# Seven block products instead of eight in two layers of an attention and expert kernel, second and third pass

## The chip, the core and the metric

One core of a Trainium2 chip runs the whole program. The metric is the device time of one execution in microseconds (us). The engines are TensorE (PE, with PEld for its weight loads), VectorE (DVE), ScalarE (ACT), GpSimd (POOL), and SyncE (SP), which issues the DMA transfers.

## What is computed

Attention over 2 x 8 heads of 768 rows of 64, masked to pairs with the same hash of six signs; its output, 1536 rows of 512, goes through two dense layers:

```python
x = attn_out.transpose(0, 2, 1, 3).reshape(1536, 512)
x = ((x @ w_a) * (x @ w_b)) @ w_out        # 512 -> 1536 -> 512, "expert layers", "expert output"
h = x @ w_in                               # 512 -> 2048, "hidden layer"
out = np.maximum(0.01 * h, h) @ w_out2     # 2048 -> 512, "last layer"
```

## The kernel before

The rows after attention are worked on in three passes of 512. The first runs between the attention tiles; the second and third come after it, with PE alone on the dense layers. Every product is made in three matmuls: each operand is split into a rounded part (fp32r, names ending in h) and the rest (names ending in l), and h·h, l·h and h·l are accumulated (`three`, L710, and `out_products`, L797). A weight unit is 128 x 512 numbers; `weights` (L361) loads it from a copy in DRAM (`kept`), rounds it on ACT or DVE (`wh`), and subtracts on DVE or POOL (`wl`).

`moe` (L735) computes, per pass, 12 pairs of blocks of the expert layers (24 x 12 matmuls), gates and splits them (`gh`, `gl`), and then the expert output, 4 blocks of 36 matmuls; `moe2` (L783) the hidden layer, 16 blocks of 12 with a leaky relu, split into `hh` and `hl`, and the last layer, 16 chunks of 12. All these matmuls stream 512 columns. Results stand in six PSUM banks (`psM`, `psN`) used in turn.

Nothing is issued by hand: `Plan` (L41) collects operations with engine, estimated length and due time, and `issue` (L103) orders them once, at build time; rings (`RINGS`) limit how many buffers of a name are alive. Each engine then runs its own list in that order and waits on semaphores.

Of the kernel before, what the change touches and what calls it, by code (L numbers as in the profile page):

```python
# [19 lines left out]
UT = 256  # L20
# [7 lines left out]
}  # L28


# [6 lines left out]
    "LATE": 10, "STIR": 24, "by": {"act": -610.0, "dve": 16.0, "pool": -157.0},  # L37
}


# [156 lines left out]
def lsh_attention_moe_kernel(  # L197
# [34 lines left out]
    wp = ctx.enter_context(tc.tile_pool(name="wp", bufs=1))  # L232

    NA = 2 * NB
    eye = const.tile([128, 128], F32, name="eye")
# [91 lines left out]

    first = list(w_units())
    NU = len(first)
    kept = [dram.tile([128, 512], F32, name="kept%d" % i) for i in range(NU)] if wide else None  # L330

    plan = Plan()
    op = plan.op
    T, P = {}, {"wp": wp}
    SP, PE, ACT, DVE, POOL = "sp", "pe", "act", "dve", "pool"
    eng = {DVE: dve, POOL: pool}

# [23 lines left out]
    def alloc(*news):  # L361
        return [n for n, _ in news], lambda f: (lambda *e: ([m() for _, m in news], f(*e)))

    def weights(i, b, at):
# [3 lines left out]
        if wide and b == 0:  # L368
# [30 lines left out]
            def f_add():  # L399
# [19 lines left out]
            op(SP, 360, lambda: sp.dma_start(out=kept[i], in_=T["w32", k]), at - 8500, "keep",  # L419
               reads=[("w32", k)], writes=[("kept", i)], uses=[("w32", k)], lag=3500)  # L420
        else:
            n, f = alloc(w32)
# [283 lines left out]
    def tick(ns):  # L706
        clock["at"] += ns * clock["pace"]
        return clock["at"]

    def three(ps, w, x, reads, uses, first, last, new_ps):  # L710

        for kt in range(4):
            def emit(kt=kt):
                hi, lo = (T[k].rearrange("p (c f) -> p c f", c=4)[:, kt] for k in w)
                mh, ml = x(kt)
                o = T[ps]
                pe.matmul(o, hi, mh, start=first and kt == 0, stop=False)  # L717
                pe.matmul(o, hi, ml, start=False, stop=False)  # L718
                pe.matmul(o, lo, mh, start=False, stop=last and kt == 3)  # L719

            nn, f = alloc(*(new_ps if kt == 0 else []))
            op(PE, 3 * MM, f(emit), tick(3 * MM), "m" if kt == 0 else None,
               reads=list(w) + reads(kt), writes=[ps], new=nn,
               uses=list(w) + uses + ([] if nn else [ps]))

    def two(names, p, pool, n, ring=None):

# [2 lines left out]

    def bank_m(ring, key):
        r = next(ring)
        return [new(r, [128, 512], F32, key, "m", r)]

    def moe(p, ring, x_reads):  # L735
        unit = iter(range(NU))
# [46 lines left out]
    def moe2(p, ring):  # L783
        unit = iter(range(NU - 2 * KH, NU))
        yh, yl, hh, hl = ((x, p) for x in ("yh", "yl", "hh", "hl"))
        for f in range(KH):
            w = weights(next(unit), p, clock["at"])
            ps, tk = ("ph", p, f), ("h32", p, f)
            three(ps, w, lambda kt: (T[yh][:, kt], T[yl][:, kt]),
                  lambda kt: [yh + (kt,), yl + (kt,)], [yh, yl], True, True,  # L790
                  bank_m(ring, ps))
            op(ACT, 600, lambda ps=ps: act.activation(T[ps], T[ps], AF.Lrelu, alpha=0.01),
               clock["at"], reads=[ps], writes=[tk], uses=[ps])
            split(ps, tk, hh, hl, f, two(("hh", "hl"), p, "h", KH) if f == 0 else [], True)
        NT = PT // 128

        def out_products(f, i, w):  # L797
            ps, ts = ("po", p, i), slice(i * 128, (i + 1) * 128)

            def emit():  # L800
                wh, wl = T[w[0]], T[w[1]]
                pe.matmul(T[ps], T[hh][:, f, ts], wh, start=f == 0, stop=False)  # L802
                pe.matmul(T[ps], T[hh][:, f, ts], wl, start=False, stop=False)  # L803
                pe.matmul(T[ps], T[hl][:, f, ts], wh, start=False, stop=f == KH - 1)  # L804

            nn, al = alloc(*(bank_m(ring, ps) if f == 0 else []))
            op(PE, 3 * MM, al(emit), tick(3 * MM), "m", reads=list(w) + [hh + (f,), hl + (f,)],
               writes=[ps], new=nn, uses=list(w) + [hh, hl] + ([] if nn else [ps]))

        LAST = KH - 2  # L810
        for f in range(LAST):
            w = weights(next(unit), p, clock["at"])
            for i in range(NT):
                out_products(f, i, w)
        ws = {f: weights(next(unit), p, clock["at"] + (f - LAST) * 3 * MM)
              for f in range(LAST, KH)}
        for i in range(NT):
            for f in range(LAST, KH):
                out_products(f, i, ws[f])
            g, c = divmod(p * PT // 128 + i, KT)  # L820
            dst = out[g * S:(g + 1) * S, :].rearrange("(p c) e -> p c e", p=128)[:, c, :]
            ps, ot = ("po", p, i), ("ot", p, i)
            nn, al = alloc(new("o", [128, 512], F32, ot, "o"))
            op({ACT: 600, DVE: 690}, 0, al(lambda e, ps=ps, ot=ot: rounded(e, T[ot], T[ps])),
               clock["at"], reads=[ps], writes=[ot], new=nn, uses=[ps])
            op(SP, 600, lambda dst=dst, ot=ot: sp.dma_start(out=dst, in_=T[ot]),
               clock["at"], reads=[ot], uses=[ot], lag=2000)

    def reload(p, at):

        full, xh, xl = ("x32f", p), ("xh", p), ("xl", p)
        n, f = alloc(new("xx", [128, KX, PT], F32, full, "x32f"))
        op(SP, 600, f(lambda: sp.dma_start(out=T[full], in_=xd[p])), at, "xl",
           reads=[("xd", p, c, o) for c in range(KX) for o in range(0, PT, UT)], writes=[full],
           new=n, lag=5000)
        for c in range(KX):
            n, f = alloc(*([new("xx", [128, KX, PT], F32R, key, nm, ring=nm)
                            for key, nm in ((xh, "xh1"), (xl, "xl1"))] if c == 0 else []))
            us = [full] if n else [full, xh, xl]
            op(ACT, 630, f(lambda c=c: act.activation(T[xh][:, c], T[full][:, c], AF.Copy)),  # L840
               at + 9000, "xs", reads=[full], writes=[xh + (c,)], new=n, uses=us)
            op({POOL: 1300, DVE: 692}, 0, lambda e, c=c: eng[e].tensor_tensor(
                out=T[xl][:, c], in0=T[full][:, c], in1=T[xh][:, c].bitcast(F32),
                op=ALU.subtract), at + 10000, "xd", reads=[full, xh + (c,)], writes=[xl + (c,)],
               uses=[full, xh, xl], lock=True)


    def pools(stack, space, **bufs):
        for n, b in bufs.items():
            P[n] = stack.enter_context(tc.tile_pool(name=n, bufs=b, **space))  # L850

    with tc.manual_schedule():
        outer, right, left, psum, psb = (ExitStack() for _ in range(5))
        in_psum = {"space": PSUM}
        on_right = {"side": "right"}
        pools(outer, on_right, edge=1)
        P["edge"].tile([128, 248], F32, name="edge")
        pools(right, on_right, pw=1, raw=1, km=1, qs=1, e=1, pt=1, st=1)
        pools(left, {}, x=1, t=1, g=1)
# [42 lines left out]
        clock["at"], clock["pace"] = start2 + PAR["START"], PAR["PACE"]  # L902
        moe(0, cycle(["psM"]), xs0)

        def free_banks():
            psb.close()
            pools(psb, {**in_psum, **on_right}, psN=1, psP=1)

        def free_right():
            right.close()  # L910
            pools(right, on_right, o=1, xx=1, h=1)

        sw3 = op("host", 0, free_banks, 0, after=plan.ring_users("B") + plan.ring_users("Sa"))
        sw2 = op("host", 0, free_right, 0, after=list(range(n_att)))
        plan.ring("psN", 4, sw3)
        plan.ring("mp", 2, sw3)
        for r in ("x32f", "xh1", "xl1", "hh", "hl"):
            plan.ring(r, 1, sw2)
# [12 lines left out]
        right.close()  # L931
# [33 lines left out]
```

## Time and profile before

| | us |
|---|---|
| median of 3 runs | 815.25 (815.14 to 815.39) |
| the profiled execution | 815.48 |
| its span, first to last instruction | 813.8 |
| PE / DVE / ACT / POOL busy | 802.5 / 462.5 / 510.8 / 194.5 |
| second and third pass on PE | 440.1 to 810.1 |

A page has the engines' busy times, the span in 40 slices, DMA queues, the chain that ended last, and groups of instructions by line. An engine's busy share is an average over the span, so it is read by stretches. Matmuls are pipelined: the recorded length of one (0.39 us) is longer than the distance to the next.

### The profile page before, as it was taken

What the parts mean: (1) busy time and instruction counts of PE and PEld (TensorE: products, weight loads), DVE (VectorE), ACT (ScalarE), POOL (GpSimd) and SP (SyncE); (2) the same over time, 40 slices, a digit from 0 to 9 for tenths busy, and PEclk for the clock granted to TensorE, in tenths of its full rate; (3) what the DMA queues carried; (4) which work ended last, traced back from release to release, by engine and by line L of the source; (5) the groups of instructions that cost most, each with busy time, mean ns of one, the idle gap of its engine ahead of it and who ended that gap; (6) DMA issues with size and microseconds to landing.
All of it is one profiled execution on the core that took longest, in us unless ns stands there. A gap on an engine that the chain in (4) does not pass through costs nothing.

```text
span 813.8 us, 12310 instructions
## 1 busy us (share of the span) xinstructions
PE 802.5 (99%) x4248; PEld 657.0 (81%) x4248; DVE 462.5 (57%) x757; ACT 510.8 (63%) x969; POOL 194.5 (24%) x295
## 2 busy tenths in 40 slices
PE   7999999999999999999999999999999999999998
PEld 6787887878878778778888888888888888888886
DVE  6665776767858766568984454355422544335421
ACT  7887898888878777879864444256423444246522
POOL 3222344443544343438861000000000000000000
PEclk9999999999999999999999999999999999999999
DMA  4354664676766554578785333432334323333332
GB/s 107 91 123 125 166 182 121 180 226 212 196 179 199 166 160 155 164 237 288 258 289 181 104 91 99 148 100 95 97 98 145 101 95 100 96 99 94 100 91 77
DMA packets 96926, 118.76 MB, mean 146 GB/s; under 512 B 31936, under 2 KB 63328, under 8 KB 96608
## 3 DMA queue, kind: packets, MB, share of 16 engines
q1 hardware_dynamic: 96064, 117.78, 48.1%
q8 instruction: 33, 0.54, 0.3%
q10 hardware_dynamic: 800, 0.20, 0.1%
q14 instruction: 29, 0.24, 0.1%
HBM read 82.84 MB, written 23.07 MB: 130 GB/s over the span
## 4 chain that ended last, share of the span: by engine, by line
PE 93%; ACT 2%; DVE 2%; POOL 1%; issue 1%; DMA 0%; POOLq 0%; ACTq 0%; DVEq 0%
PE m L717 17%; PE m L718 17%; PE m L719 17%; PE S L583 8%; PE B L663 8%; PE B L621 7%; PE m L804 5%; PE m L802 5%; PE m L803 5%; PE B L520 2%; ACT e L599 1%; PE B L674 1%; DVE st L587 1%; PE B L488 1%; DMA kept<-w 0%
## 5 line engine op out<-in xcount | busy, mean ns | idle before, releaser
L341 ACT ACTIVATE wh<-w 128x512 fp32r<-128x512 f32 x188 | 118.6, 631 | 209.8 <-PE m L718 112.7
L438 DVE TENSOR_TENSOR wl<-w,wh 128x512 fp32r<-128x512 f32 x172 | 122.8, 714 | 173.6 <-ACT wh L341 173.3
L717 PE MATMUL m<-xh,wh 128*128 128x512 f32 x480 | 190.0, 396 | 1.0 <-DVE hl L778 1.0
L718 PE MATMUL m<-xl,wh 128*128 128x512 f32 x480 | 187.1, 390 | 0.0
L719 PE MATMUL m<-xh,wl 128*128 128x512 f32 x480 | 187.0, 390 | 0.0
L587 DVE TENSOR_REDUCE st<-S 128x1 f32<-128x768 f32 x96 | 91.8, 957 | 44.0 <-PE S L583 42.0
L599 ACT ACTIVATE e<-S,st 128x768 f32<-128x768 f32 x96 | 95.3, 992 | 19.9 <-POOL st L594 15.7
L400 POOL TENSOR_TENSOR w<-m,r 128x512 uint32<-128x512 uint32 x68 | 90.7, 1335 | 65.4 <-ACT r L390 22.1
L719 PEld LDWEIGHTS m<-xh,wl 128*128 128x128 f32 x480 | 90.2, 188 | 19.2
L717 PEld LDWEIGHTS m<-xh,wh 128*128 128x128 f32 x480 | 90.2, 188 | 19.0 <-DVE hl L778 1.4
L718 PEld LDWEIGHTS m<-xl,wh 128*128 128x128 f32 x480 | 90.3, 188 | 17.5
L341 ACT ACTIVATE P<-B 128x384 f32<-128x384 f32 x187 | 82.2, 489 | 16.9 <-PE B L621 16.2
L621 PE MATMUL B<-eye,e 128*128 128x128 f32 x576 | 79.3, 274 | 0.0
L802 PE MATMUL m<-wh,hh 128*128 128x512 f32 x192 | 74.7, 389 | 0.0
L803 PE MATMUL m<-wl,hh 128*128 128x512 f32 x192 | 74.7, 389 | 0.0
L804 PE MATMUL m<-wh,hl 128*128 128x512 f32 x192 | 74.7, 389 | 0.0
L621 PEld LDWEIGHTS B<-eye,e 128*128 128x128 f32 x576 | 67.1, 141 | 3.6
L663 PE MATMUL B<-P,vr 128*64 128x256 f32 x576 | 67.5, 383 | 0.0
L583 PE MATMUL S<-TH,S 128*128 128x512 f32 x192 | 55.3, 369 | 4.2 <-ACT e L599 3.8
L663 PEld LDWEIGHTS B<-P,vr 128*64 128x64 f32 x576 | 39.2, 137 | 24.6 <-DVE st L587 2.5
L717 PE MATMUL m<-gh,wh 128*128 128x512 f32 x144 | 57.5, 399 | 0.0
L718 PE MATMUL m<-gl,wh 128*128 128x512 f32 x144 | 56.2, 391 | 0.0
(95 smaller groups left out, 1084.6 us busy)
## 6 DMA issues: line engine op xcount, KB each, us to landing
w<-kept SPq DMA_DIRECT2D x136, 256.0 KB
kept<-w SPq DMA_DIRECT2D x68, 256.0 KB
w<-in_moe_w_out_dram SPq DMA_DIRECT2D x28, 512.0 KB
w<-in_moe_w_in_dram SPq DMA_DIRECT2D x16, 512.0 KB
w<-in_moe_w_a_dram SPq DMA_DIRECT2D x12, 512.0 KB
w<-in_moe_w_b_dram SPq DMA_DIRECT2D x12, 512.0 KB
S<-TH SPq DMA_DIRECT2D x28, 192.0 KB
vr<-in_v_dram SPq DMA_DIRECT2D x16, 192.0 KB
```

The source lines that it names most:

```text
L341: act.activation(out, src, AF.Copy, scale=scale)
L438: op({POOL: 1300, DVE: 692}, 0, f(lambda e: eng[e].tensor_tensor(out=T["lo", k], in0=T["w32", k], in1=T["hi", k].bitcast(F32), op=ALU.subt ...
L583: pe.matmul(T[ps][:, o:z], T[a][:rows, cs], T[m][:rows, o:z], start=(n == 0), stop=(n == 1))
L599: act.activation(T[e], T[ps][:, :S], AF.Exp, bias=x[:, 2:3], scale=x[:, 1:2], accum_out=T[sm][:, col:col + 1])
L621: pe.transpose(T[pb][:, c * 128:(c + 1) * 128], T[e][:, k0:k0 + 128], eye)
L663: pe.matmul(T[ps][64 * i:64 * i + 64, :UT], T[Vs[i]][:, c], T[Ps[i]][:, c], start=(c == 0), stop=(c == KT - 1))
L717: pe.matmul(o, hi, mh, start=first and kt == 0, stop=False)
L718: pe.matmul(o, hi, ml, start=False, stop=False)
L719: pe.matmul(o, lo, mh, start=False, stop=last and kt == 3)
L802: pe.matmul(T[ps], T[hh][:, f, ts], wh, start=f == 0, stop=False)
L803: pe.matmul(T[ps], T[hh][:, f, ts], wl, start=False, stop=False)
L804: pe.matmul(T[ps], T[hl][:, f, ts], wh, start=False, stop=f == KH - 1)
```

## The change

In passes two and three, `moe` and `moe2` are replaced by `moe_s` and `moe2_s`. The expert output and the last layer are each cut into 2 x 2 blocks, and per chunk of the contraction (6 and 8 chunks, each of two 128-blocks) seven products of sums of blocks are accumulated in seven banks instead of eight products (Strassen's algorithm in a form with 4 + 4 sums of operands and 7 of products). The names P1 to P7 below are these banks, U1 to U4 the partial sums of them; U1 is a copy of P1, U2 = P6 + U1, U4 = P5 + U2, U3 = P7 + U2, and the four results are P2 + U1, P3 + U4, P5 + U3 and U3 - P4. Each product is six matmuls of 256 columns.

The sums need the unsplit values: gated and hidden blocks go to `Fg` (two buffers, eight 256-column blocks, four of them sums), weights to `Fw` (two buffers). ACT rounds three plain blocks and four sums, DVE forms the sums and subtracts; the results are `big` for activations (8 buffers), `Wa` and `Wb` for weights (2 and 3). The expert and hidden layers take two weight units at a time through `Fw` and `Wb`. The expert output's weights are kept in DRAM in another layout (`rows`). Eight banks are used in turn, results are written from two `o` buffers (three before). In the hidden layer the third and fourth block of the input are taken first (`order`).

```diff
-    def three(ps, w, x, reads, uses, first, last, new_ps):
+    def three(ps, w, x, reads, uses, first, last, new_ps, wide_w=None, order=(0, 1, 2, 3)):
...
+    "Fw": 2, "Fg": 2, "Wa": 2, "Wb": 3, "u": 3,
...
-    def reload(p, at):
+    def reload(p, at, after=()):
...
+    def sums(e, t, left, j):
+        x = T[t]
+        if left:
+            ops = [(4, 0, 2, ALU.add), (5, 4, 1, ALU.subtract)] if j == 0 else [
+                (6, 1, 0, ALU.subtract), (7, 3, 5, ALU.subtract)]
+        else:
+            ops = [(4, 0, 1, ALU.subtract), (5, 2, 4, ALU.subtract)] if j == 0 else [
+                (6, 2, 0, ALU.subtract), (7, 5, 3, ALU.subtract)]
+        for o, a, b, f in ops:
+            eng[e].tensor_tensor(out=x[:, o], in0=x[:, a], in1=x[:, b], op=f)
...
+    def seven(layer, c, p, at):
...
+        halves_of(t, slice(1, 4), [t + (0,), t + (1,)], lambda j: T[ka][:, j], "wab",
+                  [128, 2, 3, UT], ka, "Wa", at - PAR["wah"], at - PAR["wal"], off=1)
+        combine(t, layer == "y", at - PAR["wc"])
+        halves_of(t, slice(4, 8), [t + ("c", 0), t + ("c", 1)], lambda j: T[kb][:, j], "wab",
+                  [128, 2, 4, UT], kb, "Wb", at - PAR["wbh"], at - PAR["wbl"], off=4)
...
+    def seven_products(layer, p, ring, n, banks):
+        w_left = layer == "y"
+        ws = {}
+        steps = [(c, q) for c in range(n - 2) for q in (1, 6, 5, 2, 3, 7, 4)]
+        steps += [(n - 2, q) for q in (1, 6, 5, 2, 3, 7)]
+        steps += [(n - 1, q) for q in (1, 6, 5, 2, 3, 7)] + [(n - 2, 4), (n - 1, 4)]
...
+                for z in range(2):
+                    o = T[bank][:, z * UT:(z + 1) * UT]
+                    sh, sl = (y[:, z * 128:(z + 1) * 128] for y in s)
+                    for j, (a, b) in enumerate(((sh, m[0]), (sh, m[1]), (sl, m[0]))):
+                        pe.matmul(o, a, b, start=c == 0 and z == j == 0,
+                                  stop=c == n - 1 and j == 2, skip_group_check=True)
...
+        u_add(2, P_[6], U_[1])
+        u_add(4, P_[5], U_[2])
+        yield (1, 1), P_[2], U_[1], ALU.add, add
+        yield (1, 2), P_[3], U_[4], ALU.add, add
+        u_add(3, P_[7], U_[2])
+        yield (2, 2), P_[5], U_[3], ALU.add, add
+        yield (2, 1), U_[3], P_[4], ALU.subtract, add
...
-        plan.ring("o", 3, sw2)
+        plan.ring("o", 2, sw2)
...
-        for p in range(NP):
-            at = clock["at"]
-            if p:
-                moe(p, banks, lambda kt, p=p: [("xh", p, kt), ("xl", p, kt)])
-            if p < NP - 1:
-                reload(p + 1, at + 20000 if p == 0 else clock["at"])
-            moe2(p, banks)
+        moe2(0, banks)
...
+        plan.ring("big", 8, sw5)
+        banks = cycle(["psM"] * 2 + ["mp"] * 2 + ["psN"] * 4)
+        for p in range(1, NP):
+            moe_s(p, banks)
+            moe2_s(p, banks)
```

On PE, at the joint between expert output and hidden layer, before (m is the bank, gh and gl the gated blocks, xh and xl the two parts of the next layer's input):

```order
L717 MATMUL m<-gh,wh 128x512
L718 MATMUL m<-gl,wh 128x512
L719 MATMUL m<-gh,wl 128x512
L717 MATMUL m<-xh,wh 128x512
L718 MATMUL m<-xl,wh 128x512
L719 MATMUL m<-xh,wl 128x512
```

and now, in the second pass, the last chunk's products and the first matmuls of the hidden layer (mp is a bank too):

```order
L984 MATMUL m<-Wa,big 128x256 x6
L984 MATMUL m<-Wb,big 128x256 x12
L984 MATMUL mp<-Wa,big 128x256 x12
L984 MATMUL m<-Wb,big 128x256 x18
L729 MATMUL m<-xh,Wb 128x512
L730 MATMUL m<-xl,Wb 128x512
L731 MATMUL m<-xh,Wb 128x512
```

The 512-column matmuls over gh and gl have become groups of six 256-column ones, and the two last groups are P4 of two chunks. On DVE, at the border between the hidden and the last layer of the third pass, before:

```order
L778 TENSOR_TENSOR hl<-m,hh 128x512
L438 TENSOR_TENSOR wl<-w_8095,wh 128x512
L778 TENSOR_TENSOR hl<-m,hh 128x512
L438 TENSOR_TENSOR wl<-w_8117,wh 128x512
L438 TENSOR_TENSOR wl<-w_8139,wh 128x512
```

and now, from the sums of a hidden pair (Fg) through those of a weight chunk (Fw) to the next:

```order
L873 TENSOR_TENSOR Fw<-Fw 128x256 x4
L873 TENSOR_TENSOR Fg<-Fg 128x256 x4
L890 TENSOR_TENSOR Wb<-Fw,Wb 128x1024
L890 TENSOR_TENSOR Wa<-Fw,Wa 128x768
L890 TENSOR_TENSOR big<-Fg,big 128x768
L890 TENSOR_TENSOR big<-Fg,big 128x1024
L873 TENSOR_TENSOR Fw<-Fw 128x256 x4
L890 TENSOR_TENSOR Wa<-Fw,Wa 128x768
L890 TENSOR_TENSOR big<-Fg,big 128x768
L890 TENSOR_TENSOR Wb<-Fw,Wb 128x1024
```

One residual of 512 columns per unit has become four sums and two wide residuals per chunk, and those of the activations stand between those of the weights. At the end of the program ACT had, before:

```order
L341 ACTIVATE wh<-w_8309 128x512
L341 ACTIVATE wh<-w_8327 128x512
L341 ACTIVATE wh<-w_8345 128x512
L341 ACTIVATE o<-m 128x512 x4
L960 UNCONDITIONAL_BRANCH
```

and DVE has now:

```order
L890 TENSOR_TENSOR Wb<-Fw,Wb 128x1024
L996 TENSOR_TENSOR u<-m,u 128x512 x2
L996 TENSOR_TENSOR o<-m,u 128x512 x2
L996 TENSOR_TENSOR u<-mp,u 128x512
L996 TENSOR_TENSOR o<-m,u 128x512
L996 TENSOR_TENSOR o<-u,mp 128x512
```

Four copies of finished banks have become seven dependent sums (with a copy of P1 on ACT), four of which write the output buffers.

## Rows read from the trace of the kernel before

**Rows 1.** The page: span, busy time of each engine (share, instructions), granted clock in tenths.

```profile
span 813.8 us, 12310 instructions
PE 802.5 (99%) x4248; PEld 657.0 (81%) x4248; DVE 462.5 (57%) x757; ACT 510.8 (63%) x969; POOL 194.5 (24%) x295
...
PEclk9999999999999999999999999999999999999999
```

**Rows 2.** Busy time by stretch: stretch, its length, engines (instructions), clock, DMA share, GB/s.

```profile
440.14:505.43 65.29, 65.29 (x290) 54.08 (x289) 31.48 (x47) 28.25 (x49) 0.00 (x0) 1.00 0.36 107
505.43:538.07 32.64, 32.64 (x145) 27.04 (x145) 13.81 (x21) 11.79 (x21) 0.00 (x0) 1.00 0.40 129
538.07:581.59 43.52, 43.52 (x193) 36.05 (x193) 22.07 (x32) 26.87 (x48) 0.00 (x0) 1.00 0.32 97
581.59:625.11 43.52, 43.52 (x193) 36.05 (x193) 11.10 (x16) 12.80 (x21) 0.00 (x0) 1.00 0.35 106
...
sum 369.94, PE 369.92 PEld 306.07 DVE 153.83 ACT 156.06 POOL 0.00; mean PE 46.24 PEld 38.26 DVE 19.23 ACT 19.51 POOL 0.00
```

**Rows 3.** Timeline of PE in the hidden layer, second pass: start, length, engine, line, names, shapes.

```profile
559.66 0.39 PE L717 MATMUL m<-xh,wh 128*128 128x512 f32 x1
...
565.78 0.39 PE L717 MATMUL m<-xh,wh 128*128 128x512 f32 x1
```

**Rows 4.** Timeline of PE in the attention: hash products (384) and score products.

```profile
30.60 0.51 PE L520 MATMUL B<-TH,both_l 128*128 128x384 f32 x2
30.95 0.51 PE L520 MATMUL B<-TL,both_h 128*128 128x384 f32 x2
31.30 0.52 PE L583 MATMUL S<-TH,S 128*128 128x512 f32 x2
31.65 0.52 PE L583 MATMUL S<-TL,S 76*128 76x512 f32 x2
```

**Rows 5.** Groups by form, whole span, PE and PEld: count, busy us, mean ns, idle before.

```profile
L583 PE MATMUL S<-TL,S 76*128 76x256 f32 x96 | 27.1, 282 | 0.0
...
L717 PEld LDWEIGHTS m<-xh,wh 128*128 128x128 f32 x480 | 90.2, 188 | 19.0 <-DVE hl L778 1.4
```

**Rows 6.** The page's DMA issues: the writes of weights to DRAM.

```profile
kept<-w SPq DMA_DIRECT2D x68, 256.0 KB
```

**Rows 7.** Groups by form from 450 us to the end: DVE, then ACT.

```profile
L438 DVE TENSOR_TENSOR wl<-w,wh 128x512 fp32r<-128x512 f32 x130 | 89.9, 691 | 152.3 <-ACT wh L341 152.3
...
L341 ACT ACTIVATE wh<-w 128x512 fp32r<-128x512 f32 x130 | 82.2, 632 | 192.2 <-PE m L718 102.3 <-PE m L804 54.6 <-issue 35.2
```

**Rows 8.** Groups by form, whole span: DVE with 256 columns, ACT with 768.

```profile
L277 DVE TENSOR_TENSOR both_l<-both,both_h 128x256 fp32r<-128x256 f32 x1 | 0.4, 427 | 0.0
...
L341 ACT ACTIVATE S<-TH 64x768 fp32r<-64x768 f32 x3 | 2.4, 838 | 0.1
```

**Rows 9.** Timelines of DVE, ACT and PE around the joint of the second pass.

```profile
533.71 1.29 DVE L842 TENSOR_TENSOR xl<-x32f,xh 128x512 fp32r<-128x512 f32 x2
...
539.15 0.68 DVE L768 TENSOR_TENSOR xl<-m,xh 128x512 fp32r<-128x512 f32 x1
...
538.41 0.58 ACT L341 ACTIVATE xh<-m 128x512 fp32r<-128x512 f32 x1
...
539.26 0.39 PE L717 MATMUL m<-xh,wh 128*128 128x512 f32 x1
```

**Rows 10.** Timeline of ACT at the end of the program.

```profile
806.02 0.60 ACT L341 ACTIVATE o<-m 128x512 f32<-128x512 f32 x1 [3.45 <-PE m L804]
...
810.15 0.60 ACT L341 ACTIVATE o<-m 128x512 f32<-128x512 f32 x1 [0.81 <-PE m L804]
```

**Rows 11.** DMA from 805.8 to 813.8 us in 40 slices of 0.2 us: busy tenths, GB/s.

```profile
DMA  0000000059970006996000999300099930000000
GB/s 0 0 0 0 0 0 0 0 215 379 440 277 0 0 0 266 440 379 226 0 0 0 379 389 430 113 0 0 0 379 379 440 113 0 0 0 0 0 0 0
```

**Rows 12.** Timeline of PEld in the attention: six loads of the transposes.

```profile
202.87 0.70 PEld L621 LDWEIGHTS B<-eye,e 128*128 128x128 f32 x6
```

More of the change, by code (lines that the diff above doesn't have):

```diff
@@ L808, in out_products @@
                writes=[ps], new=nn, uses=list(w) + [hh, hl] + ([] if nn else [ps]))
+        reload(p + 1, clock["at"])
         LAST = KH - 2
@@ new lines, in combine, with halves_of @@
+    def combine(t, left, at):
+        for j in range(2):
+            op({DVE: 770, POOL: 1450}, 0, lambda e, j=j: sums(e, t, left, j), at,
+               reads=[t + (0,), t + (1,)] + ([t + ("c", 0)] if j else []), writes=[t + ("c", j)],
+               uses=[t], lock=True)
+    def halves_of(t, blocks, reads, dst, pool, shape, key, ring, at, at_lo, news=True, off=0):
+        n = blocks.stop - blocks.start
+        d = slice(blocks.start - off, blocks.stop - off)
+        nn, al = alloc(*([new(pool, shape, F32R, key, ring)] if news else []))
+        us = [t] if news else [t, key]
+        op({ACT: 264 + n * 183, DVE: 154 + n * 134}, 0, al(lambda e: rounded(
+            e, dst(0)[:, d], T[t][:, blocks])), at, reads=reads, writes=[key + (d.start, 0)],
+           new=nn, uses=us, lock=True)
+        op({DVE: 159 + n * 267, POOL: 100 + n * 600}, 0, lambda e: eng[e].tensor_tensor(
+            out=dst(1)[:, d], in0=T[t][:, blocks], in1=dst(0)[:, d].bitcast(F32),
+            op=ALU.subtract), at_lo, reads=reads + [key + (d.start, 0)],
+           writes=[key + (d.start, 1)], uses=[t, key], lock=True)
@@ new lines, in of_unit, with two_units, parts, of @@
+    def of_unit(i):
+        return (kept[i], [("kept", i)]) if wide else (first[i], [])
+    def two_units(i, p, at):
+        t, k = ("Fw", i, p), ("Wb", i, p)
+        load_w(t, [of_unit(i), of_unit(i + 1)] if i + 1 < IN2 else
+               [of_unit(i), of_unit(i + KH // 2)], at - PAR["wl"])
+        halves_of(t, slice(0, 4), [t + (0,), t + (1,)], lambda j: T[k][:, j], "wab",
+                  [128, 2, 4, UT], k, "Wb", at - PAR["w2h"], at - PAR["w2l"])
+        def parts(n):
+            def of(kt):
+                return [T[k][:, j].rearrange("p b c -> p (b c)")[
+                    :, n * 512 + kt * 128:n * 512 + (kt + 1) * 128] for j in range(2)]
+            return of
+        return [k + (0, 0), k + (0, 1)], parts
@@ new lines, in moe2_s @@
+    def moe2_s(p, ring):
+        yh, yl = ("yh", p), ("yl", p)
+        yr = lambda kt: [x + (kt, j) for x in (yh, yl) for j in (1, 2)]
+        k = KH // 2
+        for c in range(k):
+            w, parts = two_units(IN2 + c, p, clock["at"])
+            t = ("Fg", "h", c, p)
+            for z in range(2):
+                ps = ("ph", p, c + z * k)
+                three(ps, w, lambda kt: (T[yh][:, kt], T[yl][:, kt]), yr, [yh, yl], True, True,
+                      bank_m(ring, ps), parts(z), (2, 3, 0, 1))
+                nn, al = alloc(*([new("F", [128, 8, UT], F32, t, "Fg")] if z == 0 else []))
+                op(ACT, 600, al(lambda ps=ps, t=t, z=z: act.activation(
+                    T[t][:, 2 * z:2 * z + 2].rearrange("p b c -> p (b c)"), T[ps], AF.Lrelu,
+                    alpha=0.01)), clock["at"], reads=[ps], writes=[t + (z,)], new=nn,
+                   uses=[ps] + ([] if nn else [t]))
+            big_of(t, ("big", "out", c, p), True, clock["at"], p)
+        if p < NP - 1:
+            reload(p + 1, clock["at"] + PAR["xr"], plan.ring_users("Fg")[-2:])
+        for (i, j), a, b, f, add in seven_products("out", p, ring, k, None):
+            ot = ("ot", p, i, j)
+            nn, al = alloc(new("o", [128, 512], F32, ot, "o"))
+            add(lambda ot=ot: T[ot], a, b, ot, nn, al, [a[0], b[0]], f)
+            g, c = divmod(p * PT // 128 + (2 - i) * 2, KT)
+            dst = out[g * S:(g + 1) * S, :].rearrange("(p c) e -> p c e", p=128)[
+                :, c:c + 2, (2 - j) * UT:(3 - j) * UT]
+            op(SP, 600, lambda dst=dst, ot=ot: sp.dma_start(
+                out=dst, in_=T[ot].rearrange("p (z e) -> p z e", z=2)), clock["at"], reads=[ot],
+               uses=[ot], lag=2000)
@@ L852, in lsh_attention_moe_kernel @@
     with tc.manual_schedule():
-        outer, right, left, psum, psb = (ExitStack() for _ in range(5))
+        outer, right, left, psum, psb, base = (ExitStack() for _ in range(6))
         in_psum = {"space": PSUM}
@@ L903, in lsh_attention_moe_kernel @@
         moe(0, cycle(["psM"]), xs0)
+        n_y = len(plan.ops)
         def free_banks():
```

181 lines of the change are left out of this document (156 added, 25 removed), and 2 rows, old and new, of the table PAR.

## The prediction

> **What bounds the kernel now.** I read the page from the top: TensorE (PE) is busy for 99% of the span, VectorE (DVE) for 57%, and the granted clock is full in every slice [rows 1]. A busy share averages over stages, so the next view is the table by stage, cut at the layer borders of the second and third pass: eight stretches from 440.14 to 810.08 us, 369.94 us in sum, PE busy in all of it, clock 1.00, DVE busy for 153.83 us and ScalarE (ACT) for 156.06 us, GpSimd (POOL) idle [rows 2]. "Busy" of PE is modelled, so I check it with starts: in a plain stretch 27 matmuls begin in 559.66 to 565.78 us, 0.2267 us each [rows 3], and a pass has 288 + 144 + 192 + 192 = 816 of them: 816 x 0.2267 = 185.0 us, twice 370.0. So the two passes are a gapless row of 512-column matmuls, and their number times their pitch is their time. Whatever takes matmul columns away is worth its full price, as long as PE never waits.
>
> **What the products save.** Of 816 matmuls per pass the change touches 336 (expert output 144, last layer 192), 336 x 0.2267 = 76.2 us. Seven products instead of eight, each cut into two halves of 256 columns: 6 x 42 + 8 x 42 = 588 matmuls of 256 columns per pass. In columns that is 7/8. In time it depends on the pitch of a 256-column matmul whose weights change every time, and before has no long row of these. The nearest: the score products, 512 and 256 columns in turn. A pair of them takes 0.35 us from start to start [rows 4]. Less 0.227 for the 512 leaves 0.123 for the 256. The piece "x2" of 0.52 us ends with a 256 of 0.282 us [rows 4, 5], so the 256 began 0.24 after the 512 and the next matmul 0.11 after the 256. A third way: 384 columns take 0.175 (30.60 to 31.30 us, four matmuls, [rows 4]); a line through 0.175 and 0.227 gives 0.123 at 256. Ends 0.110 and 0.128, and I take 0.120, between the two readings, since an uneven split of the pair only moves time between its members. 588 x 0.120 = 70.6 us per pass. Gain 5.6 us a pass, **11.2 us** in both; by the ends 23 and 2 us. One nanosecond of pitch is worth 1.2 us.
>
> The page TensorE: Matmul & The Clock Gate of the Trainium skill (Back-to-back issue gap) gives 262 cycles of the full clock for 256 columns, an estimate of 0.109 us, and 518 cycles, 0.216 us, for 512. The row has 0.2267 for 512 [rows 3], so this kernel's matmuls stand above that rule by 0.011, and by the row the sum stays at 0.120. By the rule the gain would be 24 us, which is near rival 2.
>
> **What must not be late.** The order of PE up to the end of the first pass is the same row for row, so the first 440 us stay; the only edits there are 12 of the 68 writes of weights to DRAM [rows 6], now in pieces of 512 B, whose data is read back 100 us later, and the reload of the next input, moved behind the hidden layer's products. I cost them at nothing. The reload's cover is the first pass's last layer, 192 x 0.2267 = 43.5 us; without it PE would wait for its four copies and four subtracts, 0.63 and 0.69 each [rows 7], some 5 us.
>
> The sums are new work on DVE. Per chunk and side ("set"): four sums of 256 columns, a residual of 768 and one of 1024. A 512-column subtract is busy 0.691 us, a 256-column one 0.427 [rows 7, 8], so 1.03 ns a column: 0.955 and 1.22 us for 768 and 1024. Two in a row take 1.29, the second 0.68, so they start 0.61 apart [rows 9]: 0.08 of each lies under the next where nothing is waited for. A set is 3.4 us with all overlaps, 3.9 without; every second sum reads the first, so 3.6. A pass has 28 sets (100.8 us), 20 residuals of double units (22.8), 12 gatings (7.3), 18 combinations of products (11.7), against 76.9 before for everything. What counts is the halves. From the expert layers to the expert output: 12 sets and the rest make 69 us of DVE beside 65.3 + 252 x 0.120 = 95.5 us of PE. From the second hidden layer to the end of the last: 16 x 3.6 + 8 x 1.14 + 11 x 0.65 + 2.4 = 76.3 us beside 43.5 + 40.3 = 83.8 us. So DVE turns from half idle to 91% in these halves. ACT (0.632 us for 512 columns, 0.838 for 768 [rows 7, 8], so 1.04 for 1024) has 16 x 1.88 + 8 x 1.04 + 16 x 0.58 + 4 = 52 us there, and POOL almost nothing.
>
> The narrowest place: the second piece of DVE's order. The sixth pair of hidden blocks is there 6 x 5.44 = 32.6 us into the half, plus 0.5 for the half's late start and 1.1 for the activation, 34.2. From there to the weights of the fourth chunk stand 6 groups of four sums (9.6), 7 of 1024 (8.0) and 8 of 768 (7.0): 24.6 us, ready at 58.8. PE wants them in its second product of that chunk, at 0.5 + 43.5 + 3 x 5.04 + 0.72 = 59.8. **One us of slack** on 25 of work: at 3.4 a set none is used up, at 3.9 PE waits 1 us. Before that point DVE needs 4.75 of every 5.44 us, after it 3.6 of every 5.04. I put the waits at 0.75 us a half, **1.5** in all, 0 to 5 in the range.
>
> The joint between expert output and next hidden layer: before, PE ran through it (a matmul starts at 539.26 while the last block is being split, 538.41 to 539.83 [rows 9]) since that block is used last. Now two DVE sums, two ACT copies and two residuals stand between the third product's end and the first matmul. DVE has U2, U4, two sums and two residuals in a row behind P6; counted with 0.61 to 0.69 each from P6's end (4.1 us before PE's last product) the residuals of blocks 2 and 3 end 0.3 us after that last product. PE starts with blocks 2 and 3 of four half units, 24 matmuls, 5.4 us, and blocks 0 and 1, ready after 4 us, are not waited for. Cost 0.5 us, twice: **1.0**.
>
> The end: before, the last matmul, a copy of 0.60 us at 810.15, a transfer that moves data from 811.6 to 812.4, end of span 813.8 [rows 1, 10, 11]. Now a DVE sum of 0.69 stands there, and of two output buffers the fourth result waits for the transfer of the second: that one is written about 1.2 us before PE's end, a transfer is done 1.6 us after its data (806.62 to 808.2 [rows 10, 11]), so at 0.4, and the third result before it keeps DVE until then. Cost **0.5**, at worst 1.5.
>
> Sum: 815.5 (the profiled execution; its span is 813.8, 1.7 lie around it) - 11.2 + 1.5 + 1.0 + 0.5 = 807.3. The median of the runs is 0.2 below the profiled one: **807.0 us**.
>
> **The rivals.** (1) The supply is the bound, and the kernel gets slower. The place is the two Fw buffers: a buffer is loaded (2.4 us, from 1.6 for 256 KB and 0.8 more for as much again [rows 11]), summed (1.6), rounded on ACT (1.04, with two hand-overs 1.2), subtracted (1.14): 6.3 us, and in between DVE serves the other buffer, up to 3.6. That is 9.9 us for two chunks, PE takes 10.1. If 1.2 us are added to each turn, a chunk takes 5.55 instead of 5.04: 0.5 x 28 chunks = 14 us, **820 us**. It decides against the change from 0.3 us a chunk (28 x 0.3 = 8.2). For it: two buffers, DVE at 91%, loads in SP's order behind waits for DVE. Against: the average of DVE leaves 1.4 us a chunk, the loads move 97 to 129 GB/s in these stages [rows 2] where one transfer alone reaches 440 [rows 11].
>
> (2) The short reading of the pair holds, 0.110: 152.3 - 1176 x 0.110 = 22.9 gained, **795.5 us**. Against it the line through 384 and 512. The page's gap, 0.109 by estimate, would give 794 (see above: its 512 is shorter than the row's).
>
> (3) The weight loads are not hidden. A load is recorded with 0.188 us [rows 5]: behind a 512-column matmul of 0.227 it fits, behind 256 it would set the pitch: 1176 x 0.188 = 221.1 against 152.3, with the rest 815.5 + 68.8 + 3 = **887 us**. Against it: six loads of full size in the transposes lie within 0.70 us, at most 0.117 each [rows 12]. The same page (The mechanism) says that a load overlaps a matmul in flight only where the row groups differ, which would speak for this rival; the trace does not agree, since loads of all rows stand behind every matmul at 0.2267 [rows 3, 5].
>
> (4) Columns are saved, but what is late eats it (joints and end at their upper ends, pitch 0.125): **815 us**, no change.
>
> **How the numbers follow.** Forecast 0.78 (807; 815.3 less 14.8 for a pitch of 0.117, with 2 us of waits, is 802.5, less 6.5 for 0.124, with 4.5 us, 813), rival 1 0.10, rival 2 0.04, rival 3 0.02, rival 4 0.06. The range is the forecast's own: rivals 1 to 3 and most of 4, 0.2 in all, lie outside. 0.2%, 1.6 us, is about what a measurement of this kernel can tell from no change: faster takes the forecast, rival 2 and a mild rival 1 (0.84), the same is rival 4 and the forecast's edge (0.06), slower the rest (0.10).
>
> **What would show it.** In the profile after: the starts of 256-column matmuls 0.120 apart; PE's waits in the two products stages below 1 us each, put down to DVE residuals of Wb or Wa around the fourth chunk of the last layer; DVE at 80% in the last 360 us; expert output 30.2 and last layer 40.3 us long. Wrong: a pitch of 0.13 or more; waits at every chunk behind Fw loads (rival 1); waits of several us at the joints; an end more than 4.5 us behind the last matmul.

## The result

| | before | after |
|---|---|---|
| median of 4 runs, us | 815.32 (815.14 to 815.44) | 805.36 (804.97 to 806.91) |
| profiled execution, us | 815.48 | 806.91 |
| its span, us | 813.8 | 805.2 |

The ratio is 0.9882, with a 95% interval of 0.9864 to 0.9899: 10.0 us faster by the medians, 1.6 us beyond the forecast of 807.0. The execution whose profile is read here is the longest of the four. Executions of either kernel take some 1.4 us more where the granted clock is lower from 10 to 20 us (0.85 in the profile of before, 0.83 in that of after, 1.00 in others), and at the same mean clock the two kernels differ by 8.6 to 8.7 us and not by 10.0: 815.48 to 806.91 in the profiled executions (0.997 and 0.998), 813.9 to 805.2 by the medians of those at 1.000, here and beside the experiments. The profiles come to the first pass's last layer up to 2.1 us apart (394.72 to 396.86 us), so lengths of stages are compared below, not the times at which they begin.

The page of after, beside [rows 1]: span, busy time of each engine (share of the span), the granted clock in tenths.

```profile
span 805.2 us, 13347 instructions
PE 791.4 (98%) x4752; PEld 671.7 (83%) x4752; DVE 593.4 (74%) x976; ACT 525.6 (65%) x915; POOL 199.3 (25%) x298
...
PEclk9999999999999999999999999999999999999999
```

There are 504 more matmuls, PE is busy for 11 us less, and DVE has gone from 57% to 74%. The stages of the second pass (two layers with paired units, expert output, hidden layer, last layer), and the sum over both passes, beside [rows 2]: stretch, its length, engines (instructions), clock, DMA share, GB/s.

```profile
441.53:506.81 65.28, 65.28 (x290) 54.05 (x288) 45.09 (x67) 29.59 (x37) 0.00 (x0) 1.00 0.35 112
506.81:537.04 30.23, 30.23 (x254) 30.23 (x252) 24.55 (x39) 9.60 (x12) 0.00 (x0) 1.00 0.35 106
537.04:580.63 43.59, 43.59 (x194) 36.03 (x193) 37.94 (x63) 30.99 (x41) 2.42 (x1) 1.00 0.31 97
580.63:620.95 40.32, 40.32 (x338) 40.31 (x337) 35.79 (x57) 17.27 (x22) 0.00 (x0) 1.00 0.40 140
...
sum 358.85, PE 358.85 PEld 321.21 DVE 285.16 ACT 172.06 POOL 4.83; mean PE 44.86 PEld 40.15 DVE 35.64 ACT 21.51 POOL 0.60
```

Expert output went from 32.64 to 30.23 us and the last layer from 43.52 to 40.32; the two others stayed. PE is busy in all of each stage. The starts of the block products in the last layer (timeline of PE: start, length, engine, line, names, shapes, count) give the pitch, the time from one matmul's start to the next, and the timeline of DVE gives the residual that the last of these rows needs:

```profile
592.87 1.60 PE L984 MATMUL mp<-Wa,big 128*128 128x256 f32 x12
594.30 1.60 PE L984 MATMUL m<-Wb,big 128*128 128x256 f32 x12
595.75 0.88 PE L984 MATMUL m<-Wa,big 128*128 128x256 f32 x6
596.47 1.60 PE L984 MATMUL m<-Wb,big 128*128 128x256 f32 x12
```

```profile
593.52 1.22 DVE L890 TENSOR_TENSOR Wb<-Fw,Wb 128x1024 fp32r<-128x1024 f32 x1
```

30 matmuls start in 3.60 us, one every 0.120 us, the forecast's value to the digit. The row at 596.47 is the second product of the fourth chunk, the place that the prediction called the narrowest: 580.63 + 3 x 5.04 + 0.72 = 596.47. Its weights are ready at 594.74, so 1.73 us of slack were left where one was forecast.

The joint of the second pass, PE and then DVE:

```profile
535.60 1.60 PE L984 MATMUL m<-big,Wa 128*128 128x256 f32 x12
537.04 0.39 PE L729 MATMUL m<-xh,Wb 128*128 128x512 f32 x1
537.27 0.42 PE L730 MATMUL m<-xl,Wb 128*128 128x512 f32 x1
537.52 0.39 PE L731 MATMUL m<-xh,Wb 128*128 128x512 f32 x1
```

```profile
536.44 0.69 DVE L1058 TENSOR_TENSOR xl<-m,xh 128x512 fp32r<-128x512 f32 x1
...
539.74 0.68 DVE L1058 TENSOR_TENSOR xl<-m,xh 128x512 fp32r<-128x512 f32 x1
```

The residuals of blocks 2 and 3 end at 537.13, those of blocks 0 and 1 at 540.42. The first matmul, at 537.04, reads xh alone; the first that needs a residual (xl) starts at 537.27. It lasts 0.03 us longer than its neighbours, and the whole stage takes 43.59 us where it took 43.52, so the joint costs 0.07 us at most.

The end of the program; PE, DVE and SP, beside [rows 10, 11], and the last matmul of before:

```profile
809.68 0.39 PE L804 MATMUL m<-wh,hl 128*128 128x512 f32 x1
```

```profile
798.22 2.32 PE L984 MATMUL mp<-Wb,big 128*128 128x256 f32 x18
```

```profile
797.73 1.38 DVE L996 TENSOR_TENSOR o<-m,u 128x512 f32<-128x512 f32 x2
...
800.62 0.69 DVE L996 TENSOR_TENSOR o<-m,u 128x512 f32<-128x512 f32 x1 [0.80 <-DMA out_dram<-o]
801.40 0.69 DVE L996 TENSOR_TENSOR o<-u,mp 128x512 f32<-128x512 f32 x1
```

The last matmul starts at 798.22 + 17 x 0.120 = 800.26, and the span ends 4.9 us later, 4.1 before. The third result waits 0.80 us for a buffer that the first result's transfer holds, and the fourth queues behind it.

The one loss at a place costed at nothing is in the first pass's last layer, DVE and then PE:

```profile
408.81 3.59 DVE L857 TENSOR_TENSOR xl<-Fg,xh 128x512 fp32r<-128x512 f32 x4
...
413.64 0.69 DVE L448 TENSOR_TENSOR wl<-w,wh 128x512 fp32r<-128x512 f32 x1
```

```profile
412.73 0.39 PE L815 MATMUL m<-wh,hh 128*128 128x512 f32 x1
414.38 0.50 PE L816 MATMUL m<-wl,hh 128*128 128x512 f32 x1 [1.26 <-DVE wl L448]
```

The four subtractions of the reloaded input, moved here by the change, hold DVE for 3.59 us; the weight residual that stands behind them on DVE ends at 414.33, and PE's next matmul starts 1.65 us after the last one instead of 0.23. The layer takes 45.19 us (396.34 to 441.53) where it took 43.52.

### The profile page after: what moved, and what is told of

Same layout as the page of the kernel before. It is cut to its first block, busy times and chain, and to the rows that moved or that the text cites. A ratio compares the mean times of both kernels' runs of the same rounds, so it can differ in the third digit from the quotient of the medians.

```text
span 805.2 us, 13347 instructions
## 1 busy us (share of the span) xinstructions
PE 791.4 (98%) x4752; PEld 671.7 (83%) x4752; DVE 593.4 (74%) x976; ACT 525.6 (65%) x915; POOL 199.3 (25%) x298
## 5 line engine op out<-in xcount | busy, mean ns | idle before, releaser
L346 ACT ACTIVATE Wb<-Fw 128x1024 fp32r<-128x1024 f32 x62 | 65.2, 1056 | 58.9 <-PE m L731 17.3
L730 PE MATMUL m<-xl,Wb 128*128 128x512 f32 x240 | 93.5, 389 | 0.0
L729 PE MATMUL m<-xh,Wb 128*128 128x512 f32 x240 | 93.4, 389 | 0.0
L731 PE MATMUL m<-xh,Wb 128*128 128x512 f32 x240 | 93.4, 389 | 0.0
L890 DVE TENSOR_TENSOR Wb<-Fw,Wb 128x1024 fp32r<-128x1024 f32 x66 | 80.5, 1221 | 13.9 <-ACT Wb L346 13.5
L729 PE MATMUL m<-xh,wh 128*128 128x512 f32 x160 | 65.4, 409 | 1.0 <-DVE hl L791 1.0
L730 PE MATMUL m<-xl,wh 128*128 128x512 f32 x160 | 62.6, 391 | 0.0
L731 PE MATMUL m<-xh,wl 128*128 128x512 f32 x160 | 62.5, 390 | 0.0
L890 DVE TENSOR_TENSOR big<-Fg,big 128x1024 fp32r<-128x1024 f32 (+1 forms) x56 | 59.0, 1087 | 2.8 <-ACT big L346 2.8
L346 ACT ACTIVATE big<-Fg 128x768 fp32r<-128x768 f32 (+1 forms) x54 | 50.4, 944 | 5.0 <-DVE Fg L873 4.8
L730 PEld LDWEIGHTS m<-xl,Wb 128*128 128x128 f32 x240 | 45.1, 188 | 9.4
```

The source lines that it names most:

```text
L346: act.activation(out, src, AF.Copy, scale=scale)
L729: pe.matmul(o, hi, mh, start=first and n == 0, stop=False)
L731: pe.matmul(o, lo, mh, start=False, stop=last and n == 3)
L890: op({DVE: 159 + n * 267, POOL: 100 + n * 600}, 0, lambda e: eng[e].tensor_tensor(out=dst(1)[:, d], in0=T[t][:, blocks], in1=dst(0)[:, d]. ...
```

## Experiments

**Is the pitch the price of the products?** One of the seven products is issued twice:

```diff
...
+                if q == 2:
+                    for z in range(2):
+                        o = T[bank][:, z * UT:(z + 1) * UT]
+                        sh, sl = (y[:, z * 128:(z + 1) * 128] for y in s)
+                        for j, (a, b) in enumerate(((sh, m[0]), (sh, m[1]), (sl, m[0]))):
+                            pe.matmul(o, a, b, start=False,
+                                      stop=c == n - 1 and j == 2, skip_group_check=True)
```

> The third block product of every chunk is issued twice, so that its result is not the one wanted: 48 matmuls a chunk instead of 42, 14 chunks a pass, two passes, so 168 more matmuls of 256 columns; nothing else is touched. Theory (TensorE's pitch of 120 ns is all that bounds the block products): +168 x 0.120 = +20.2 us, 825.6 us against 805.4. Rival (the supply of chunks has its own pace near that of TensorE): part of the 20 us is absorbed, under +15 us. What it prices as well: this is the count of an ordinary block product, eight in place of seven, with all the sums still there.

Measured 827.1 us, span 825.4 against 805.2. Expert output and last layer of the second pass:

```profile
506.90:541.45 34.55, 34.55 (x289) 34.55 (x288) 24.89 (x39) 9.51 (x12) 0.00 (x0) 1.00 0.31 92
...
585.01:631.08 46.07, 46.07 (x385) 46.06 (x384) 36.12 (x57) 17.02 (x22) 0.00 (x0) 1.00 0.39 123
```

34.55 = 6 x 48 x 0.120 and 46.07 = 8 x 48 x 0.120; 20.2 us for 168 matmuls, as the theory had it. It tells more than that: eight products in 256-column pieces are slower than what stood there before (34.55 against 32.64, 46.07 against 43.52), since two matmuls of 256 columns take 0.240 us and one of 512 takes 0.2267. Of the 12.5% that the algebra saves, 5.1 points go to the smaller pieces: 7/8 of the columns take 92.6% of the time (588 x 0.120 against 336 x 0.2267).

**What sets 0.120?** From the second chunk on, fewer columns are streamed (224, then 160), and then also fewer weight columns loaded:

```diff
+                        if c:
+                            o, b = o[:, :160], b[:, :160]
```

```diff
+                        if c:
+                            o, a, b = o[:64, :160], a[:, :64], b[:, :160]
```

> From the second chunk of each stage of block products on, the matmuls stream 224 of the 256 columns; the last 32 columns of each are left out. 1008 of the 1176 matmuls are shortened. Theory 1 (a fixed part beside the columns): 512 columns took 226.7 ns and 256 take 120 ns, so a column takes 0.4167 ns and 13.4 ns are fixed; 224 columns take 106.7 ns, and the time falls by 1008 x 13.4 ns = 13.5 us to 791.9 us. Theory 2 (the load of each matmul's own weights sets the 120 ns): the pitch stays at 120 ns and the time at 805.4 us.

> As the run with 224 columns, but 160 of 256 columns are streamed and 96 left out. Theory 1 (fixed part of 13.4 ns, columns at 0.4167 ns): a pitch of 80.1 ns in stretches without a wait; if the supply of chunks can follow, -1008 x 39.9 ns = -40 us, 765 us. Theory 2 (weight loads set a floor): the pitch stops at a floor between 80 and 120 ns, the same as or near the one at 224 columns. Rival 3 (supply): a chunk would take 42 x 0.080 = 3.4 us on TensorE, while VectorE alone needs 0.95 + 1.55 + 1.22 = 3.7 us for it; then waits stand between the chunks and a chunk takes 4 us or more, and the time falls by less than 30 us.

> As the run with 160 columns, where the pitch stopped at 111.5 ns as it did at 224 columns, and with 64 in place of 128 weight columns loaded for each of these matmuls (half of the output rows and 96 of 256 columns are left out). Theory (the floor is the load of the weights, 128 columns long, of which one stands before every matmul): the floor falls with the weight columns, the pitch in stretches without a wait is set by the 160 streamed columns, about 80 ns, and the chunks then wait for VectorE (3.5 us of each against 42 x 0.080 = 3.4), so that the time is some 770 to 785 us. Rival (a floor of 111.5 ns for any matmul with weights of its own, whatever their size): 111.5 ns and 798 us again.

Measured 798.2, 798.2 and 792.6 us. Timelines of PE in the last layer of the three, in this order:

```profile
761.91 1.50 PE L986 MATMUL mp<-Wb,big 128*128 128x224 f32 x12
763.25 0.84 PE L986 MATMUL m<-Wa,big 128*128 128x224 f32 x6
```

```profile
766.56 1.50 PE L986 MATMUL mp<-Wb,big 128*128 128x160 f32 x12
767.90 0.83 PE L986 MATMUL m<-Wa,big 128*128 128x160 f32 x6
```

```profile
594.25 1.04 PE L986 MATMUL mp<-Wa,big 128*64 128x160 f32 x12
595.13 1.04 PE L986 MATMUL m<-Wb,big 128*64 128x160 f32 x12
...
597.47 1.02 PE L986 MATMUL m<-Wb,big 128*64 128x160 f32 x11 [0.78 <-DVE Wb L890]
```

1.34 / 12 = 0.112 with 224 columns and the same with 160: the straight line through 512 and 256 breaks off, so theory 1 falls, and theory 2 in its plain form too, since 0.112 is below 0.120. With 64 weight columns, the 160 columns take 0.88 / 12 = 0.073. The floor goes with the weight columns that are loaded, so it is put down to the load: 0.112 for 128 columns, just under the 0.120 that 256 streamed columns take. (The same edit halves the rows of the result, and no run parts the two.) The page TensorE: Matmul & The Clock Gate of the Trainium skill (LDWEIGHTS) gives the number of weight columns over 1.2 in ns, an estimate of 107 ns for 128; the floor stands 5 ns above that. The last kernel came out at 792.6 us where 770 to 785 was expected: with PE quicker, DVE set the pace in many chunks (from the fourth to the eighth in the second pass's last layer), as the last row shows, and the saved time went into such waits, and in part into stretches in which the granted clock was 0.50 (from 702 to 708 us, for one).

**How much slack has the supply?** The sums are computed twice, all four or one of the four of a set:

```diff
-        for o, a, b, f in ops:
+        for o, a, b, f in ops + ops[:2]:
```

```diff
-        for o, a, b, f in ops:
+        for o, a, b, f in ops + (ops[:1] if j == 0 else []):
```

> Every one of the four sums that are made of a set of blocks (weights and inputs alike) is computed twice: about 1.6 us more on VectorE for each of the 28 + 28 sets of the two passes, some 90 us of VectorE in all; results as before. Theory of the prediction (about 1 us of slack in the 24.6 us of VectorE ahead of the fourth chunk's weights): the added 6 to 8 us there show as stalls of TensorE at the start of each of the four stages of block products, +10 to +25 us in all. Rival (the sets are made far enough ahead, by the buffers of Wb and big, and slack is several us at each place): under +2 us.

> One of the four sums of each set is computed twice: 0.42 us more on VectorE for each of the 56 sets of the two passes, 23 us in all; results as before, and the order of the instructions is the same. With all four doubled the time was 862.4 us. Theory A (what counts is VectorE's idle time in a stage: in the hidden layer and the last layer together it was busy 73.8 of 84.0 us, so 10.2 us are free, and 16 sets x 0.42 = 6.7 us fit in; in the expert output 6 sets, 2.5 us, into 5.7 us free): no change, 804 to 807 us. Theory B (of the prediction: about 1 us of slack ahead of the fourth chunk's weights): the 2 us added to that chain show as some 1 us per stage, 4 us in all, 809 to 811 us.

Measured 862.4 and 807.3 us. Doubled, the three stages of the second pass from expert output on:

```profile
505.24:546.10 40.86, 34.51 (x254) 33.49 (x252) 37.94 (x70) 11.03 (x14) 0.00 (x0) 0.92 0.27 84
546.10:589.67 43.57, 43.57 (x194) 36.05 (x193) 39.59 (x76) 25.18 (x34) 2.41 (x1) 1.00 0.26 85
589.67:648.88 59.21, 45.92 (x338) 43.61 (x337) 57.62 (x108) 22.85 (x29) 0.00 (x0) 0.94 0.31 99
```

Both theories were too small for it. DVE is busy for 57.62 of the 59.21 us of the last layer: not a chain but the whole engine has become the bound. Its work in hidden and last layer was 37.94 + 35.79 = 73.7 us; 16 sets with four sums more, 1.47 us by their starts, make it 97.2, which is the sum of 39.59 and 57.62, and the two stages now last 102.8 where PE's own work takes 84. With one sum doubled, PE and DVE at the fourth chunk of the last layer:

```profile
594.40 0.28 PE L984 MATMUL m<-Wb,big 128*128 128x256 f32 x1
595.47 1.58 PE L984 MATMUL m<-Wb,big 128*128 128x256 f32 x11 [0.78 <-DVE Wb L890]
```

```profile
594.19 1.22 DVE L890 TENSOR_TENSOR Wb<-Fw,Wb 128x1024 fp32r<-128x1024 f32 x1
```

The stage began at 578.16, so this residual ends 17.25 us into it; in after it ended 14.11 us into it. The 3.1 us that were added are 1.73 of slack and 1.4 of waiting (0.3 of it already at the third chunk, behind a residual of Wa), and the stage is 41.76 us long instead of 40.32 (41.77 in the third pass). Expert output kept its 30.23. So theory A, which looked at idle time in a stage, is wrong here: 10 us were idle, and 6 to 7 more of work did not fit. Theory B had the right place but put waits in four stages where two had them, and its 809 to 811 us were too many.

**Are two Fw buffers needed, and do they do?**

```diff
-    "Fw": 2, "Fg": 2, "Wa": 2, "Wb": 3, "u": 3,
+    "Fw": 1, "Fg": 2, "Wa": 2, "Wb": 3, "u": 3,
```

> One buffer for the weights as loaded, Fw, in place of two; results as before, the planner puts some instructions elsewhere. A buffer is held from the issue of its load to its last residual: some 2.1 us for the transfer, 1.5 us for the four sums, 1.05 us for the copy to Wb and 1.22 us for its residual, one behind the other, about 6.3 us with what lies between. Theory (with one buffer the chunks come every 6.3 us, where TensorE takes 5.04; with two they may take 10.1 us, and so two are enough): 28 chunks x 1.3 us = +36 us less what the stages' starts have in hand, some 835 to 845 us, with TensorE's waits at every chunk. Rival 1 of the prediction (two buffers are at the edge already): then one buffer makes every chunk wait for several us more, and the time goes past 880 us.

Measured 905.7 us, more than either. One turn of the buffer in the expert output, SP and DVE:

```profile
522.95 0.52 SPq L905 DMA_DIRECT2D Fw<-rows  x1
```

```profile
521.70 1.23 DVE L890 TENSOR_TENSOR Wb<-Fw,Wb 128x1024 fp32r<-128x1024 f32 x1 [0.31 <-ACT Wb L346]
527.52 1.55 DVE L873 TENSOR_TENSOR Fw<-Fw 128x256 f32<-128x256 f32 x4 [4.60 <-DMA Fw<-rows]
```

The next load is issued when the residual ends, and DVE has its data 4.57 us later, not 2.1 as expected (2.4 in the prediction). A turn is then 8.3 us, and the chunks of that stage come every 8.3 us (49.71 us for six). The last layer took 61.41 us, 7.7 a chunk, and the layers with paired units, taken as free, grew too (71.32 and 47.17 us). Two buffers allow 10.08 us for a turn of 8.3, so rival 1 was nearer than it looked: its load was priced at half of what it takes in the expert output. Why it did not come true all the same was only argued, not tried by itself: DVE's work for the other buffer lies inside the wait for the load and is not added to it, as the rival's sum had it.

**What hides the joint?**

```diff
-                      bank_m(ring, ps), parts(z), (2, 3, 0, 1))
+                      bank_m(ring, ps), parts(z), (0, 1, 2, 3))
```

> The hidden layer of the second and third pass reads its four input blocks in the order 0, 1, 2, 3 in place of 2, 3, 0, 1, so that TensorE begins with the two blocks which the block products deliver last; results as before. In the changed kernel the residuals of those two end at 540.42 us, where TensorE asked for the second matmul's input at 537.27. Theory (the order with which the sums are delivered and read is what hides the joint): a stall of 3 us at each of the two joints, +6 us, 811 us, and the order of other instructions shifts a little. Rival (the joint was short anyway): under +1 us.

Measured 817.6 us, span 815.6. PE at the joint, and the stretches around it (length, PE, PEld, DVE, ACT, POOL, clock):

```profile
536.28 1.60 PE L984 MATMUL m<-big,Wa 128*128 128x256 f32 x12
540.43 0.50 PE L729 MATMUL m<-xh,Wb 128*128 128x512 f32 x1 [2.55 <-ACT xh L346]
541.16 0.50 PE L730 MATMUL m<-xl,Wb 128*128 128x512 f32 x1 [0.23 <-DVE xl L1058]
```

```profile
540.40:542.24 1.84, 1.58 (x5) 1.05 (x6) 1.83 (x3) 0.00 (x0) 0.07 (x1) 0.97 0.36 81
542.24:545.23 2.99, 2.99 (x8) 2.31 (x7) 0.00 (x0) 0.00 (x0) 0.00 (x0) 0.50 0.87 282
545.62:549.00 3.38, 3.38 (x16) 2.82 (x15) 0.69 (x2) 1.10 (x3) 0.00 (x0) 1.00 0.01 4
```

The wait is 2.7 + 0.5 us, the 3 us expected. The second price was not expected: after it the granted clock is 0.50, the 1.2 GHz level, from 542.24 on, and seven matmuls take 0.427 each, 1.4 us in all, before it is back at 1.00. A joint costs 4.9 us in all (stages of 32.94 and 45.76 us against 30.23 and 43.59), two of them 9.8, and the rest of the 10.4 between the spans lies in the first pass. So the order of the blocks is worth more than the forecast of its cost.

**The two losses that remain.** First the reload's subtractions, due 6 us later; then the last two results into the free Fg buffers:

```diff
-                op=ALU.subtract), at + 10000, "xd", reads=[full, xh + (c,)], writes=[xl + (c,)],
+                op=ALU.subtract), at + 16000, "xd", reads=[full, xh + (c,)], writes=[xl + (c,)],
```

```diff
-            nn, al = alloc(new("o", [128, 512], F32, ot, "o"))
+            big = p == NP - 1 and i == 2
+            nn, al = alloc(new("F", [128, 8, UT], F32, ot, "Fg") if big else
+                           new("o", [128, 512], F32, ot, "o"))
...
```

> The four subtractions that make the low part of the reloaded input are due 6 us later, so that VectorE's order in the first pass's last layer has three weight residuals ahead of them; all else is left. Theory (the stall of TensorE at 412.7 us, 0.5 to 1.5 us long in the profiles of the changed kernel and its variants, is the weight residual queued behind these 3.6 us of VectorE): no stall there, and 0.5 to 1.5 us less than the changed kernel, 804 us. Rival (the residual is late because its weights come late, behind the reload's own transfer): the stall stays and the time is the same, 805.4 us.

> The third and fourth result block of the third pass are written into the free two buffers of Fg, so that four buffers stand for the results at the end in place of two; nothing else moves. Theory (the third sum waited 0.80 us for the first result's transfer, and the last sum queued behind it, at 801.40 us, 1.0 us after TensorE's last matmul): the last sum starts at 800.6 us and the end comes 0.8 us earlier, 804.6 us. Rival (the transfers to memory set the end, one behind the other): under 0.3 us.

> Both corrections together: the reload's subtractions due 6 us later in the first pass, and the third and fourth result block of the third pass in the free buffers of Fg. Theory (the two are independent: one took a stall of 0.5 to 1.5 us out of the first pass's last layer, the other 0.8 us out of the end, where TensorE's last matmul and the profile's end stood 4.9 us apart and then 4.1): 1.3 to 2.3 us less than the changed kernel measured beside it, about 803.7 us. Rival (what is taken out at one place is given back, since the transfers of the end run into each other): under 0.5 us.

> The changed kernel once more, unaltered, beside the one with both corrections and on the same chip: 805.4 us as before, 804.5 to 807; the profile again with a stall of TensorE between 0.5 and 1.5 us near 412 us, and with 4.9 us from the last matmul to the end.

Medians of 4: 804.71 us (803.90 to 805.19; ratio to before 0.9875, 0.986 to 0.989) for the first and 805.06 (804.15 to 806.41; 0.9876, 0.986 to 0.9893) for the second. Measured beside the changed kernel, both together took 804.64 (803.76 to 805.32; 0.9879, 0.9864 to 0.9893) and the changed kernel 806.10 (805.08 to 806.58; 0.9893, 0.9876 to 0.9909): these intervals overlap, so what each is worth is read from the stages. DVE with the later subtractions, then the end with the other buffers:

```profile
412.24 0.77 DVE L448 TENSOR_TENSOR wl<-w,wh 128x512 fp32r<-128x512 f32 x1
412.93 2.99 DVE L857 TENSOR_TENSOR xl<-Fg,xh 128x512 fp32r<-128x512 f32 x3
```

```profile
799.45 0.69 DVE L996 TENSOR_TENSOR u<-mp,u 128x512 f32<-128x512 f32 x1
800.17 0.69 DVE L996 TENSOR_TENSOR Fg<-m,u 128x512 f32<-128x512 f32 x1
800.88 0.69 DVE L996 TENSOR_TENSOR Fg<-u,mp 128x512 f32<-128x512 f32 x1
```

With the residual ahead of the subtractions the layer takes 43.52 us, as before the change, with no wait: the stall was the queue on DVE. (The planner also gave one of the four subtractions to POOL there, so that three are left on DVE, 2.99 us instead of 3.59.) With four result buffers the wait of 0.80 is gone and the span ends 4.1 us after the last matmul's start (800.57), as before the change. With both, the end is 4.1 again, but the layer takes 44.31, with a wait of 0.65 us at 416.97 behind a residual that the subtractions now precede; the changed kernel measured beside it took 44.64. DVE's and POOL's order is the same as with the later subtractions alone, but PE began the layer 1.1 us earlier (395.21 against 396.30) while the subtractions came at nearly the same time (412.81, 412.93). So the end's 0.8 us is secure, and the place in the first pass is moved to an edge rather than mended.

## Why the prediction was right

- **Bound by matmuls times pitch.** Right. Forecast 11.2 us, measured 11.0 with what the joints cost: from the first matmul of the second pass to the last of all it was 369.7 us (439.98 to 809.68) and is 358.7 (441.53 to 800.26). The value between the two readings of the pair [rows 4, 5] was right to a nanosecond, and that was luck as well as judgement: the upper end of 0.128 is worked out from no row, the line through 384 and 512 gave 0.123, and the reason given for 0.120 was drawn from another part of the kernel. The load of 0.112 lies so near below that a slightly slower one would have set another pitch. Rival 2 (0.110) was therefore out of reach: the load alone is 0.112.
- **Rival 3.** The recorded length of a load, 0.188 [rows 5], is not what it costs: loads follow each other every 0.112. Its reason (a load fits only behind a long matmul) was sound, the number was not.
- **Supply.** Forecast 1.5 us, measured 0. The place and the mechanism were right, as the quarter's run showed; the slack was 1.73 us, not 1, because a set takes DVE 3.5 us instead of 3.6 (1.47 for the four sums, 0.87 and 1.13, by the starts of such rows). So this term failed in size only, and a margin of 1.7 us on a stage of 40 held.
- **Joints.** Forecast 1.0, measured 0.14 at most. The prediction has "the residuals of blocks 2 and 3 end 0.3 us after that last product", and takes it that PE waits for them. They end at 537.13, 0.1 us after PE goes on from the last product at 537.04, and PE does not wait even so, since its first matmul reads no residual: the first that does starts at 537.27. That the delivery order and the reading order must agree was right, at 4.9 us a joint.
- **End.** Forecast 0.5, measured 0.8, by the kind of wait that was named, one place earlier: the prediction has the fourth result wait for the second's transfer, but it is the third that waits for the first's, and the fourth queues behind it. The sign of being wrong that was named for this place, an end more than 4.5 us behind the last matmul, did show (4.9 us from its start).
- **The first 440 us.** Costed at nothing; measured 1.6 in the profiled execution (1.1 in the other profile of the same kernel, 44.64 against 43.52; 0.7 to 2.3 in those of the variants that leave this place alone). PE's order was the same, and the prediction took that and a long enough cover for sufficient ("The reload's cover is the first pass's last layer"). The cover hides the reload from PE, but the reload stands in DVE's queue ahead of weight residuals which PE wants 1 us later. This is the step that was wrong. That the sum came out near all the same is luck, since this miss of 1.6 stands against 2.4 that the supply and the joints did not take: -11.0 + 0.8 + 1.6 = -8.6, which is 813.8 to 805.2, where -8.2 was forecast.

That the median came out 1.6 us below 807.0 is mostly not the change's doing: compared at the same mean clock (see the result) the change is worth 8.6 to 8.7 us where 8.2 was forecast.

## What to carry to other kernels

A block algorithm that trades products for sums pays by pitch, not by columns: price the smaller matmul, with its weight load as a floor, before the algebra, and ask whether the engine that makes the sums still fits into what is left of the stage. Slack is to be read at the one chunk where the supply is latest; two stages with 10 us idle on VectorE had 1.7 us of it there. A moved helper has to be looked at on every queue that it enters: hidden from TensorE as a whole, it can still stand ahead of the one small operation that TensorE wants next.

## What the runs showed of the hardware

With 128 weight columns loaded for each matmul the pitch stopped at 0.112 us, for 224 and 160 streamed columns alike, and with 64 weight columns 160 streamed columns came every 0.073 us. By that floor, blocks of 128 columns, which no run here has, would gain 7% of a matmul's time at most, an estimate, and not half.

Waits of PE of 2.7 and 0.5 us at a joint were followed by a stretch at the 1.2 GHz level in which seven matmuls took 0.427 us each; the wait of 1.4 us in the first pass was not (granted clock 1.00 from 414.4 us on). The length of a wait does not tell by itself: in the run with 64 weight columns, idle times of 0.71 and 1.35 us, a few matmuls apart, were followed by a clock of 0.50 in the third pass (from 767 us on) and by 1.00 in the second (from 593.4 us on).
